# Seven products in the third block too, retention in one place from the sixth on, other PSUM banks for y, and SyncE's DMAs of the second block in another order

## The chip, the core and the metric

One core of a Trainium2 chip runs the kernel. The metric is the device time of one execution in microseconds (us). Five engines work beside each other, each with its own queue in program order: TensorE (PE, with its weight loads as PEld), VectorE (DVE), ScalarE (ACT), GpSimd (POOL) and SyncE (SP). SP computes nothing here; it issues nearly all DMAs.

## What is computed

Two layers, one behind the other. The first is a retention over 4 batches, 8 heads, 768 positions and a head size of 64; the second multiplies by `w_in` (512 x 2048), applies Mish, and multiplies by `w_out` (2048 x 512):

```python
for t in range(S):
    state = gamma[None, :, None, None] * state + np.einsum('bhd,bhe->bhde', k[:, :, t], v[:, :, t])
    y[:, :, t] = scale * np.einsum('bhd,bhde->bhe', q[:, :, t], state)
...
h = x @ w_in
sp = np.where(h > 20.0, h, np.log1p(np.exp(np.minimum(h, 20.0))))
g = h * np.tanh(sp)
return (g @ w_out).astype(np.float32)
```

Here `x` is `y` with the heads side by side: 3072 rows of 512. Inputs and output are float32; the products run in float16 with float32 sums.

## The kernel before, in words

**Chunks and blocks.** The positions are cut into 24 chunks of 128 (six to a batch). `BLOCKS` (L37) groups them: block 0 has chunks 0 to 3, and block b from 1 to 10 has chunks 2b+2 and 2b+3, so 256 rows of the output. Everything for a block b happens in one round of the loop at L817, in which the retention of block b+1 is put between the matrix products of block b.

**One chunk's way.** SP loads q, k and v of a chunk (`load`, L131; 256 KB each, buffers for 4 chunks of q and 6 of k and v). POOL casts them (`casts`, L217): q times a factor (L223), k times a constant (L228), v times a factor (L229); q and k share a tile `qk16` with 4 buffers. SP then issues a DMA transpose of that tile (`turn_by_dma`, L233 to L236), which gives `qkt`. `next_chunk` (L781) does this for one chunk and issues loads some chunks ahead.

**Retention of a pair of chunks.** `get_ready` (L465) has PE make the outer products `u_ps` (L401, from the casts) and the scores `at` (L394, from `qkt`), and then `settle` (L450) runs on DVE: `mid` (L436/L438), `suh` and `sth` (L445, L447), `mid` of the second chunk, and the masked scores `am` (L459). `leave` (L470) makes the last state. `retain` (L501) has PE write the past's part of `y_ps` (L475), and DVE reads one column of it (`seen`, L514) before `finish` (L519) adds the present's part and copies y to `xt` (L526 on DVE, L528 on ACT), the input of the next block's first product. With `later` given, `retain` also makes the outer products and scores of the block after the next in between the past's matmuls: that is "retention in one place".

**The two products of a block.** `g1` (L532) makes h in 8 steps of 8 matmuls of 256 columns (L541), and ACT applies Mish (L549). Blocks below `SEVEN` then make the second product plainly: 8 steps of 4 matmuls of 512 columns (L555), with `g2_out` (L559) copying the result to `osb` on DVE (L561). Blocks from `SEVEN` on cut the second product into 2 x 2 pieces and form it from seven products of 8 matmuls of 256 columns instead of eight (`seven`, L615; matmuls L635). This needs sums of pieces of `w_out` (`weight_sums`, L572: eight DVE instructions L588 to L591, made once, one after each step of the block before), sums of pieces of g for each block (`sums_a`, `sums_b`, `sums_c`: `gsum`, L604 to L613), three copies of partial results on ACT (`snap`, L641), and four additions or copies into `osb` on DVE (L647, L649).

**Order.** It is written by hand: `tc.manual_schedule()` keeps the program's order on each engine, and `plan_of` (L791) says after which step u of a block which piece of the other work is issued. `store_due` (L176) issues the stores of `osb` (L179) ahead of a step, when they are due. Before the change block 1 has `next_chunk` after steps 1 and 5, `get_ready` after 10, `retain` after 13, `finish` and `leave` after 14. Block 2 (the block before `SEVEN`) has them after 2, 8, 7, 12 and 13. Blocks from `SEVEN` (3) to `ONE` (6) have `get_ready` and `leave` after step 3, and `retain` and `finish` between the seven products; blocks above `ONE` have only `settle` and `leave`, after step 0.

**PSUM.** Three pools share eight banks: `mmps` (tag mm, 3 buffers), `pxps` (tag px, one) and `atps` (tag at, two of two banks each). `get_ready` takes both buffers of `atps`, one for `at`, one for `u_ps`. In blocks 1 and 2 y takes the buffer of `at` next, so it must wait until `am` has been read from there.

Of the kernel before, what the change touches and what calls it, by code (L numbers as in the profile page):

```python
# [10 lines left out]
FP32 = mybir.dt.float32  # L11
# [5 lines left out]
def kernel(  # L17
# [9 lines left out]
    nc = tc.nc  # L27
    B, H, S, D = q.shape
    d_model, d_ff = moe_w_in.shape
    P = 128  # L30
# [3 lines left out]
    HP = H // 2  # L34
# [3 lines left out]
    first = [sum(BLOCKS[:i]) for i in range(len(BLOCKS))]  # L38
# [26 lines left out]
    mmps = ctx.enter_context(  # L65
        tc.tile_pool(name="rn_mmps", bufs=3, space=bass.MemoryType.PSUM))
    pxps = ctx.enter_context(
        tc.tile_pool(name="rn_pxps", bufs=1, space=bass.MemoryType.PSUM))
    atps = ctx.enter_context(
        tc.tile_pool(name="rn_atps", bufs=2, space=bass.MemoryType.PSUM))  # L70
# [40 lines left out]
    loaded, cast, qkts, ats, ams, states, mids, us, ys = {}, {}, {}, {}, {}, {}, {}, {}, {}  # L111
    xts, gts, wins, wouts, wtmps = {}, {}, {}, {}, {}
    gtiles, tmats, gsums = {}, [], []
    SEVEN, ONE = 3, 6
    nload, ncast = [0], [0]
    stores = []

# [13 lines left out]
    def load(g):  # L131
        room(g)
        for n in range(3):
            load_one(g, n, nc.sync)

    def load_to(g):
        while nload[0] < min(g, NCK):
            load(nload[0])
            nload[0] += 1
# [249 lines left out]
    def pair_tile(pool, name, tag):  # L389
        return pool.tile([P, 2, 2, HP, D], FP32, name=name, tag=tag)  # L390
# [16 lines left out]
    def hold(blk):  # L407
        held[blk] = [pair_tile(atps, nm, "at") for nm in ("at", "u_ps")]
# [12 lines left out]
    def run(*streams):  # L421
        streams = [iter(x) for x in streams]
        while streams:
            for x in list(streams):
                fns = next(x, None)
                if fns is None:
                    streams.remove(x)
                else:
                    for fn in fns:
                        fn()  # L430
# [49 lines left out]
    def past_of(blk):  # L480
        a = first[blk]
        for j in range(2):
            qt = qkts[a + j][0]
            for s in range(2):
                st = mids[a + j] if s else states[a + j - 1] if (a + j) % NCH else None
                for i in range(HP) if st is not None else ():
                    yield [
                        lambda st=st, qt=qt, i=i, j=j, s=s, hh=hh: y_mm(
                            blk, i, hh, j, s, st[half(hh), i], qt[half(hh), i, half(s)])
                        for hh in range(2)]  # L490
# [10 lines left out]
    def retain(blk, later=None, spread=False):  # L501
        if spread:
            ys[blk] = [
                mmps.tile([P, 2, HP, D], FP32, name="y_ps", tag="mm") for _ in range(2)]
        else:
            y = pair_tile(atps, "y_ps", "at")
            ys[blk] = [y[:, s] for s in range(2)]
        if later is None:
            run(past_of(blk))
        else:  # L510
            hold(later)
            run(past_of(blk), ready(later, False))

        nc.vector.tensor_copy(seen, ys[blk][1][:, 1, 0, :1])  # L514
        if later is not None:
            run(ready(later, True))
            finish(blk, False)
# [40 lines left out]

    def g2_out(o_ps, blk, t, due, cols=slice(None)):  # L559
        osb = op.tile(list(o_ps.shape), FP32, name="osb", tag="osb")  # L560
        nc.vector.tensor_copy(osb, o_ps)  # L561
        if blk == 0:
            dst = out[:TB].rearrange("(p r) c -> r p c", r=CPB)[t]
        else:
            row0 = (first[blk] + t) * P
            dst = out[row0:row0 + P, cols]
        stores.append((due, dst, osb))
# [39 lines left out]
    def sums_b(blk):  # L607
        (_, _, s3, _), a11, _, a21, _ = sum_views(blk)
        nc.vector.tensor_tensor(s3, a11, a21, op=ALU.subtract)

    def sums_c(blk):
        (_, s2, _, s4), _, a12, _, _ = sum_views(blk)
        nc.vector.tensor_tensor(s4, a12, s2, op=ALU.subtract)  # L613

    def seven(blk, hooks, last):  # L615
        n, hf = NFB // 2, d_model // 2
        px = pxps.tile([P, hf], FP32, name="o_ps", tag="px")
        pb = mmps.tile([P, hf], FP32, name="o_ps", tag="mm")
        osb = [op.tile([P, d_model], FP32, name="osb", tag="osb") for _ in range(2)]

        def a(i, j):
            return lambda f: gts[blk, j * n + f][:, i * P:(i + 1) * P]

        def b(i, j):
            return lambda f: wouts[(i * n + f) // FPS][:, f % FPS, j * hf:(j + 1) * hf]

        def s(i):
            return lambda f: gsums[blk % 2][:, i - 1, f]

        def t(i):  # L630
            return lambda f: tmats[(i - 1) // 2][:, (i - 1) % 2, f]

        def mm(o_ps, x, w, first=False):
            for f in range(n):
                nc.tensor.matmul(  # L635
                    o_ps, x(f), w(f), start=first and f == 0, stop=f == n - 1,
                    skip_group_check=True)

        def snap(o_ps):
            x = op.tile([P, hf], FP32, name="snap", tag="snap", bufs=3)  # L640
            nc.scalar.copy(x, o_ps)  # L641
            return x

        def done(i, j, o_ps, plus=None):
            dst = osb[i][:, j * hf:(j + 1) * hf]
            if plus is None:
                nc.vector.tensor_copy(dst, o_ps)  # L647
            else:
                nc.vector.tensor_tensor(dst, o_ps, plus, op=ALU.add)  # L649
            row0 = (first[blk] + i) * P  # L650
            if last:
                nc.sync.dma_start(out[row0:row0 + P, j * hf:(j + 1) * hf], dst)

        mm(px, a(0, 0), b(0, 0), True)
        m1 = snap(px)
        mm(pb, a(0, 1), b(1, 0), True)
        sums_b(blk)
        done(0, 0, pb, m1)
        pe = mmps.tile([P, hf], FP32, name="o_ps", tag="mm")
        mm(pe, s(1), t(1), True)  # L660
        m5 = snap(pe)
        mm(px, s(2), t(2))
        u2 = snap(px)
        for fn, *args in hooks[0]:
            fn(*args)
        sums_c(blk)
        mm(px, s(3), t(3))
        done(1, 1, px, m5)
        for fn, *args in hooks[1]:
            fn(*args)  # L670
        mm(pe, s(4), b(1, 1))
        done(0, 1, pe, u2)
        mm(px, a(1, 1), t(4))
        done(1, 0, px)
        if not last:
            for i in range(2):
                row0 = (first[blk] + i) * P
                stores.append((1 + i, out[row0:row0 + P], osb[i]))
# [99 lines left out]
            for fn, *args in plan.get(u + 1, ()):  # L778
                fn(*args)

    def next_chunk(g):  # L781
        if g < NCK:
            cast_to(g + 1)
            turn_by_dma(g)
            if g < first[ONE] + 5:
                load_to(g + 3 if g < first[ONE] + 2 else g + 4)
            else:
                cast_to(g + 2)
                load_to(g + 5)

    def plan_of(blk):  # L791
        a = first[blk] + 4
        if blk >= SEVEN:
            plan = {u: [] for u in (0, 1, 3, 4, 7)}
            if blk > ONE:
                if blk + 1 < len(BLOCKS):
                    plan[0] = [(settle, blk + 1), (leave, blk + 1)]
            else:
                plan[3] = [(get_ready, blk + 1), (leave, blk + 1)]
            if blk >= ONE:  # L800
                plan[1] = [(next_chunk, a + 1)]
            else:
                ua, ub = (0, 4) if blk == ONE - 1 else (1, 7)
                plan[ua] += [(cast_to, a + 1), (next_chunk, a)]
                plan[ub] += [(cast_to, a + 2), (next_chunk, a + 1)]
            return plan
        early, then_seven = blk == 1, blk + 1 == SEVEN
        plan = {1: [(cast_to, a + 1)],
                (1 if early else 2 if then_seven else 4): [(cast_to, a + 1), (next_chunk, a)],
                (5 if early else 8): [(cast_to, a + 2), (next_chunk, a + 1)]}  # L810
        plan[10 if early else 7] = [(get_ready, blk + 1)]
        plan[13 if early else 12] = [(retain, blk + 1)]
        plan[14 if early else 13] = [(finish, blk + 1), (leave, blk + 1)]
        return plan

    first_block()
    for blk in range(1, len(BLOCKS)):  # L817
        n1 = NFB * BLOCKS[blk] // CPB
        last = blk + 1 == len(BLOCKS)
        plan = plan_of(blk)  # L820
        extra = weight_sums(0) + weight_sums(1) if blk + 1 == SEVEN else []
        for u in range(n1 if blk >= SEVEN else 2 * n1):
# [5 lines left out]
            else:  # L828
                t, part = divmod(u - n1, 4)
                if part == 0:  # L830
                    o_ps = mmps.tile([P, d_model], FP32, name="o_ps", tag="mm")
# [47 lines left out]
```

## Time and profile before

| what | value |
|---|---|
| median of 3 runs (lowest, highest) | 209.09 us (207.99, 209.56) |
| profiled execution: its time, its span | 208.58 us, 206.5 us |
| granted TensorE clock | 1.00 |
| PE busy | 198.6 us, 96% of the span |
| DVE, ACT, POOL busy | 118.7, 84.6, 79.2 us |
| second product, plain (L555), 128 matmuls | 30.0 us |
| second product, seven (L635), 192 and 128 matmuls | 24.0 and 15.3 us |
| DMA moved | 38.68 MB; 96704 packets of SP's queue |

The span runs from the first to the last instruction; the time is some 2.1 us longer. The page of the profile gives each engine's busy time, the DMA queues, and the chain of waits, which follows the execution back from its last instruction to what released each step. The timelines list the instructions of an engine in order of time (start, length, engine, line, operation, output<-inputs, count), with the idle time before a group and what ended it in square brackets. For a DMA, SP's row is the issue alone; when its data have landed is told apart, in the rows of its line.

### The profile page before, as it was taken

The numbers are of one execution on the slowest core, as the hardware profiler recorded it, in microseconds if no ns is written. First come the engines' busy times: TensorE is split into PE (matmuls) and PEld (weight loads), VectorE is DVE, ScalarE is ACT, GpSimd is POOL, SyncE is SP. The second block draws the span as 40 slices with busy tenths as digits, with TensorE's granted clock in tenths as the row PEclk, the third lists the DMA queues.
The fourth block names the chain that finished last, engine by engine and source line by source line (L and its number), as shares of the span: only waits on it lengthen the run. The fifth ranks groups of instructions, "written<-read, shape, count | busy, mean of one in ns | idle before, by whom it ended". The sixth has DMA issues, their size and how long they took to land.

```text
span 206.5 us, 5987 instructions
## 1 busy us (share of the span) xinstructions
PE 198.6 (96%) x2605; PEld 147.5 (71%) x2605; DVE 118.7 (57%) x211; ACT 84.6 (41%) x149; POOL 79.2 (38%) x82
## 2 busy tenths in 40 slices
PE   7999999999998899999999999999999999999993
PEld 2555444454864674788888887888888888888873
DVE  2697454267107999476388298296863853555152
ACT  2244665043530450352453452453363453542630
POOL 3246000426867266774466595098920000000000
PEclk9999999999999999999999999999999999999999
DMA  5999999999899999999999999999990500201102
GB/s 177 236 216 344 380 387 355 231 296 204 177 209 281 187 199 207 212 186 255 244 197 215 167 219 237 173 186 230 215 196 3 152 3 3 102 3 54 51 25 76
DMA packets 99993, 38.68 MB, mean 187 GB/s; under 512 B 90496, under 2 KB 94080, under 8 KB 99968
## 3 DMA queue, kind: packets, MB, share of 16 engines
q1 hardware_dynamic: 96704, 37.50, 89.0%
q10 hardware_dynamic: 3264, 0.81, 2.3%
q8 instruction: 20, 0.33, 0.7%
q14 instruction: 5, 0.04, 0.1%
HBM read 27.29 MB, written 6.29 MB: 163 GB/s over the span
## 4 chain that ended last, share of the span: by engine, by line
PE 75%; DVE 9%; DMA 6%; SPq 6%; ACT 1%; issue 1%; DVEq 0%; ACTq 0%
PE h_ps L541 37%; PE o_ps L635 22%; PE o_ps L555 8%; SPq L128 5%; PE y_ps L475 4%; DMA wi<-in_moe_w_in_dram 3%; DMA kf<-in_k_dram 3%; DVE gsum L604 2%; DVE am L459 2%; PE u_ps L401 2%; DVE sth L447 1%; DVE mid L438 1%; PE at L394 1%; DVE suh L445 1%; DVE gsum L605 1%
## 5 line engine op out<-in xcount | busy, mean ns | idle before, releaser
L541 PE MATMUL h_ps<-xt,win 128*128 128x256 f16 (+1 forms) x704 | 86.3, 282 | 1.1 <-ACT xt L528 0.5
L541 PEld LDWEIGHTS <-win 128*128 128x128 f16 x704 | 68.4, 98 | 17.3 <-issue 1.7
L549 ACT ACTIVATE g<-h_ps 128x512 f16<-128x512 f32 x96 | 57.3, 597 | 47.6 <-PE h_ps L541 47.6
L223 POOL TENSOR_TENSOR qk<-qf,qvs 128x512 f16<-128x512 f32 x20 | 22.1, 1107 | 50.0 <-DMA qf<-in_q_dram 34.0
L229 POOL TENSOR_TENSOR v<-vf,qvs 128x512 f16<-128x512 f32 x24 | 25.5, 1064 | 17.1 <-DMA vf<-in_v_dram 15.6
L555 PE MATMUL o_ps<-wout,g 128*128 128x512 f16 x128 | 30.0, 380 | 0.0
L228 POOL TENSOR_SCALAR qk<-kf 128x512 f16<-128x512 f32 x18 | 28.0, 1555 | 3.5 <-DMA kf<-in_k_dram 2.1
L635 PEld LDWEIGHTS <-gsum 128*128 128x128 f16 x256 | 23.9, 98 | 4.7 <-DVE gsum L604 1.1
L635 PE MATMUL o_ps<-tmat,gsum 128*128 128x256 f16 x192 | 24.0, 273 | 0.7 <-ACT snap L641 0.5
L555 PEld LDWEIGHTS <-g 128*128 128x128 f16 x128 | 11.7, 98 | 12.6
L635 PEld LDWEIGHTS <-g 128*128 128x128 f16 x192 | 18.8, 98 | 2.2
L604 DVE TENSOR_TENSOR gsum<-g 128x512 f16<-128x512 f16 x16 | 9.7, 603 | 14.2 <-ACT g L549 14.2
L528 ACT CAST xt<-y_ps 128x512 f16<-128x512 f32 x12 | 6.7, 588 | 25.7 <-DVE xt L526 16.0
L641 ACT COPY snap<-o_ps 128x256 f32<-128x256 f32 x24 | 8.9, 373 | 18.0 <-PE o_ps L635 18.0
L649 DVE TENSOR_TENSOR osb<-o_ps,snap 128x256 f32<-128x256 f32 x24 | 10.1, 422 | 9.1 <-ACT xt L528 3.1
L635 PE MATMUL o_ps<-wout,g 128*128 128x256 f16 x128 | 15.3, 273 | 0.0
L438 DVE TENSOR_TENSOR mid<-u_ps,sth 128x256 f16<-128x256 f32 x15 | 6.4, 423 | 10.7 <-PE u_ps L401 10.4
L249 PE MATMUL at<-ident 128*128 128x512 f16 (+1 forms) x34 | 10.8, 448 | 1.4 <-POOL ident L84 1.4
L459 DVE TENSOR_TENSOR am<-at,tri_half 128x1024 f16<-128x1024 f32 x9 | 10.9, 1214 | 0.0
L447 DVE TENSOR_TENSOR sth<-suh,gch 128x256 f16<-128x256 f32 x15 | 9.7, 649 | 0.6
L226 ACT ACTIVATE qk<-kf 128x512 f16<-128x512 f32 x6 | 3.8, 631 | 12.4 <-DMA kf<-in_k_dram 12.4
L436 DVE CAST mid<-u_ps 128x256 f16<-128x256 f32 x3 | 1.3, 422 | 12.9 <-PE u_ps L401 12.9
(79 smaller groups left out, 175.0 us busy)
## 6 DMA issues: line engine op xcount, KB each, us to landing
kf<-in_k_dram SPq DMA_DIRECT2D x23, 256.0 KB, 5.5
vf<-in_v_dram SPq DMA_DIRECT2D x23, 256.0 KB, 5.3
out_dram<-osb SPq DMA_DIRECT2D x22, 256.0 KB, 4.6
qf<-in_q_dram SPq DMA_DIRECT2D x19, 256.0 KB, 5.1
wt<-in_moe_w_out_dram SPq DMA_DIRECT2D x3, 1024.0 KB, 10.1
wi<-in_moe_w_in_dram SPq DMA_DIRECT2D x4, 512.0 KB, 7.2
wi<-in_moe_w_in_dram SPq DMA_DIRECT2D x2, 1024.0 KB, 10.8
qfirst<-in_q_dram SPq DMA_DIRECT2D x2, 512.0 KB, 4.9
```

The source lines that it names most:

```text
L128: queue.dma_start(loaded[g][n], (q, k, v)[n][b, :, c * C:(c + 1) * C].rearrange("h p d -> p h d"))
L223: nc.gpsimd.tensor_tensor(q16, qf, qs.unsqueeze(2).broadcast_to((P, H, D)), op=ALU.mult)
L228: nc.gpsimd.tensor_scalar(k16, kf, BOOST, None, op0=ALU.mult)
L229: nc.gpsimd.tensor_tensor(v16, vf, vs.unsqueeze(2).broadcast_to((P, H, D)), op=ALU.mult)
L249: nc.tensor.matmul(ats[g][:, 0, :m], ident, ident.unsqueeze(1).broadcast_to((P, m, P)), start=True, stop=True)
L447: nc.vector.tensor_tensor(st, su, gch, op=ALU.mult)
L459: nc.vector.tensor_tensor(am.rearrange("p a j i c -> p (a j i) c"), at.rearrange("p a j i c -> p (a j i) c"), tri_half.unsqueeze(1).broadc ...
L541: nc.tensor.matmul(h_ps[:, j], wins[s][f // 2][:, bp, f % 2 * P:(f % 2 + 1) * P], xts[blk][:, bp, :nt], start=(bp == 0), stop=(bp == NBP - 1))
L549: nc.scalar.activation(gt, h_ps, AF.Mish, scale=inv_boost3)
L555: nc.tensor.matmul(o_ps, gts[blk, fb][:, t * P:(t + 1) * P], wouts[s][:, f, cols], start=(fb == 0), stop=(fb == NFB - 1))
L604: nc.vector.tensor_tensor(s1, a21, a22, op=ALU.add)
L635: nc.tensor.matmul(o_ps, x(f), w(f), start=first and f == 0, stop=f == n - 1, skip_group_check=True)
```

## The change

Six things change; the line numbers are those of the kernel before.

1. `SEVEN` goes from 3 to 2: block 2 uses the seven products, and the eight weight sums are issued in block 1 instead of block 2. With this block 2 takes the plan of the blocks that follow it: `get_ready` of block 3 after step 3.
2. `ONE` goes from 6 to 5: block 5 makes the outer products and scores of block 7 inside its `retain`, and block 6 has no `get_ready`. Block 4 takes the plan that block 5 had; from chunk 14 on, loads are issued further ahead.
3. `retain` of block 1 (the only plain one left) puts y into one buffer of `mmps` and the one of `pxps` instead of `atps`.
4. In block 1 `g2_out` copies the first of the two results on ACT instead of DVE.
5. In block 1 chunk 8's transpose is issued after step 0, so ahead of the four stores of block 0, and without loads behind it; the load of chunk 10, the transpose of chunk 9 and the load of chunk 11 follow after step 2.
6. In the last block the product that gives `u2` is made before the one in `pe`.

SP's order in block 1 is thus: transpose 8, four stores, load 10, transpose 9, load 11, where it was four stores, transpose 8, load 10, transpose 9, load 11. On POOL the casts keep their order; on DVE the eight sums stand between the last `osb` copies of block 0 and `mid` of chunk 6.

```diff
--- before.py
+++ after.py
@@ -111,7 +111,7 @@
     loaded, cast, qkts, ats, ams, states, mids, us, ys = {}, {}, {}, {}, {}, {}, {}, {}, {}
     xts, gts, wins, wouts, wtmps = {}, {}, {}, {}, {}
     gtiles, tmats, gsums = {}, [], []
-    SEVEN, ONE = 3, 6
+    SEVEN, ONE = 2, 5
     nload, ncast = [0], [0]
     stores = []
 
@@ -503,8 +503,9 @@
             ys[blk] = [
                 mmps.tile([P, 2, HP, D], FP32, name="y_ps", tag="mm") for _ in range(2)]
         else:
-            y = pair_tile(atps, "y_ps", "at")
-            ys[blk] = [y[:, s] for s in range(2)]
+            ys[blk] = [
+                pool.tile([P, 2, HP, D], FP32, name="y_ps", tag=tag)
+                for pool, tag in ((mmps, "mm"), (pxps, "px"))]
         if later is None:
             run(past_of(blk))
         else:
@@ -558,7 +559,10 @@
 
     def g2_out(o_ps, blk, t, due, cols=slice(None)):
         osb = op.tile(list(o_ps.shape), FP32, name="osb", tag="osb")
-        nc.vector.tensor_copy(osb, o_ps)
+        if blk > 0 and t == 0:
+            nc.scalar.copy(osb, o_ps)
+        else:
+            nc.vector.tensor_copy(osb, o_ps)
         if blk == 0:
             dst = out[:TB].rearrange("(p r) c -> r p c", r=CPB)[t]
         else:
@@ -657,10 +661,14 @@
         sums_b(blk)
         done(0, 0, pb, m1)
         pe = mmps.tile([P, hf], FP32, name="o_ps", tag="mm")
+        if last:
+            mm(px, s(2), t(2))
+            u2 = snap(px)
         mm(pe, s(1), t(1), True)
         m5 = snap(pe)
-        mm(px, s(2), t(2))
-        u2 = snap(px)
+        if not last:
+            mm(px, s(2), t(2))
+            u2 = snap(px)
         for fn, *args in hooks[0]:
             fn(*args)
         sums_c(blk)
@@ -778,15 +786,14 @@
             for fn, *args in plan.get(u + 1, ()):
                 fn(*args)
 
-    def next_chunk(g):
+    def next_chunk(g, loads=True):
         if g < NCK:
             cast_to(g + 1)
             turn_by_dma(g)
-            if g < first[ONE] + 5:
-                load_to(g + 3 if g < first[ONE] + 2 else g + 4)
-            else:
+            if g >= first[ONE] + 5:
                 cast_to(g + 2)
-                load_to(g + 5)
+            if loads:
+                load_to(g + (3 if g < first[ONE] + 2 else 4 if g < first[ONE] + 5 else 5))
 
     def plan_of(blk):
         a = first[blk] + 4
@@ -804,14 +811,11 @@
                 plan[ua] += [(cast_to, a + 1), (next_chunk, a)]
                 plan[ub] += [(cast_to, a + 2), (next_chunk, a + 1)]
             return plan
-        early, then_seven = blk == 1, blk + 1 == SEVEN
-        plan = {1: [(cast_to, a + 1)],
-                (1 if early else 2 if then_seven else 4): [(cast_to, a + 1), (next_chunk, a)],
-                (5 if early else 8): [(cast_to, a + 2), (next_chunk, a + 1)]}
-        plan[10 if early else 7] = [(get_ready, blk + 1)]
-        plan[13 if early else 12] = [(retain, blk + 1)]
-        plan[14 if early else 13] = [(finish, blk + 1), (leave, blk + 1)]
-        return plan
+        return {0: [(cast_to, a + 1), (next_chunk, a, False)],
+                2: [(load_to, a + 3), (cast_to, a + 2), (next_chunk, a + 1)],
+                10: [(get_ready, blk + 1)],
+                13: [(retain, blk + 1)],
+                14: [(finish, blk + 1), (leave, blk + 1)]}
 
     first_block()
     for blk in range(1, len(BLOCKS)):
```

## The prediction

> Blocks (0 to 10) and chunks (0 to 23) are counted as the code counts them; block b from 1 on holds chunks 2b+2 and 2b+3, and times are us from the start of the span of the profiled execution.
>
> **What bounds the kernel now.** I read first the page's busy shares and slices: PE is busy 96% at a granted clock of 1.0 throughout, but the DMA row stands at 9 tenths as well until about 150. So I went on to the chain of waits for the length of each block on PE, then to SP's timeline with the landing times of its transposes, because PE can only be sped up where its data are there.
>
> The chain of waits (start, length, what) gives the blocks by the start of their first h_ps:
>
> ```profile
> 51.61 7.15 PE h_ps L541 x64
> ...
> 65.39 0.56 PE y_ps L475 x24
> ...
> 68.79 7.15 PE h_ps L541 x64
> ...
> 84.82 3.49 PE h_ps L541 x32
> ...
> 99.87 3.49 PE h_ps L541 x32
> ...
> 114.84 3.49 PE h_ps L541 x32
> ...
> 130.58 3.49 PE h_ps L541 x32
> ...
> 146.19 6.99 PE h_ps L541 x64
> ```
>
> Block 1 takes 17.18, block 2 16.03, block 3 15.05, block 4 14.97, block 5 15.74, block 6 15.61, and block 7 14.52 (its neighbour starts at 160.71). Blocks 3 on have seven products; 7 on have the retention in one place.
>
> SP's timeline around blocks 1 and 2 (start, length of the issue, line, kind):
>
> ```profile
> 59.42 1.50 SPq L128 DMA_DIRECT2D vf<-in_v_dram  x1
> 61.02 2.55 SPq L179 DMA_DIRECT2D out_dram<-osb  x4
> 63.66 2.53 SPq L235 DMA_TRANSPOSE qkt<-qk  x1
> 66.24 0.57 SPq L128 DMA_DIRECT2D qf<-in_q_dram  x1
> 66.91 1.27 SPq L128 DMA_DIRECT2D kf<-in_k_dram  x1
> 68.23 0.78 SPq L128 DMA_DIRECT2D vf<-in_v_dram  x1
> 69.10 2.40 SPq L235 DMA_TRANSPOSE qkt<-qk  x1
> ```
>
> SP has no gap. The transpose at 69.10 is chunk 9's; the row of its line in that window says when it landed:
>
> ```profile
> L235 SPq DMA_TRANSPOSE qkt<-qk x1: 2396/2396/2396, 69.1 to 69.1; - x1
> ...
> DMA to landing us min/median/max: 6.9/6.9/6.9
> ```
>
> So it landed at 76.0. PE's scores of block 3 (get_ready, which reads it) began at 76.14: 0.1 to spare. The table by windows (us, PE, PEld, DVE, ACT, POOL, PEclk, DMA share, GB/s) shows that the transfers, not the issues, were the limit:
>
> ```profile
> 60.00:64.00 4.00, 4.00 (x81) 2.01 (x79) 2.02 (x4) 0.00 (x0) 2.65 (x4) 1.00 1.11 268
> 64.00:66.00 2.00, 1.32 (x29) 0.77 (x27) 1.94 (x4) 0.00 (x0) 1.92 (x2) 1.00 1.04 352
> 66.00:68.00 2.00, 2.00 (x40) 0.94 (x39) 0.72 (x2) 0.00 (x0) 0.22 (x1) 1.00 1.32 86
> 68.00:72.00 4.00, 3.48 (x32) 2.87 (x30) 3.93 (x8) 2.18 (x4) 1.19 (x1) 1.00 1.29 221
> ```
>
> The share is over 1 in every window; from 66 to 68, with the transpose behind the four stores, only 86 GB/s moved.
>
> **Block 2 with seven products.** It loses 32 matmuls o_ps of 512 columns (4.42 for 20 in the chain, so 7.07) and gains 56 of 256 (3.49 for 32, so 6.10): 0.97 less PE work, and the 15.0 of blocks 3 and 4 in place of 16.03. ACT's three snaps (0.37 each) lie beside PE as in block 3. But get_ready of block 3 moves from step 7, between the two products, to step 3, four h_ps groups (3.6) earlier, and its scores need chunk 9's transpose.
>
> **Block 1 on PE.** y goes to other banks: the 0.68 of idle ahead of the y_ps row at 65.39 (released by DVE am, whose bank it took) goes; late next is nothing, as mid of chunk 7 is done at 64.20 and PE comes at 64.7. The present part then waits only for am (65.33) and runs behind the 4 o_ps, at 66.0 to 66.4. The two xt copies, one after the other before (DVE 67.43, ACT 68.15, released by DVE), run side by side as they do from separate tiles at 98.10 in block 3, so the 0.52 ahead of 68.79 goes too. Block 2 would start at about 67.3, 1.5 earlier. The first osb copy on ACT is bounded by xt (0.59) and snap (0.37): 0.6 in ACT's idle stretch of 8.76, and it takes 0.68 off DVE behind am. The second stays behind xt, suh and sth on DVE, done near 68.9; its bank is asked for by block 2's fourth h_ps group at 69.9: nothing.
>
> **The eight weight sums,** from block 2 to block 1: DVE is idle from 52.4 to 61.81 (the row before mid says 9.44). In block 2 the eight took 6.7 for seven and 1.51 for the last, 0.69 alone and up to 1.53 beside POOL; so about 8.2, done near 60.6, before the chain of mid at 61.8. POOL pays: its casts at 70.81 took 1.53, 1.81, 1.28 against 1.04, 1.49, 1.04 alone. The same 0.35 each on five casts (chunk 7 and two of chunk 8) less the 0.99 that POOL was idle at 57.48 puts chunk 8's k cast at 60.9 instead of 60.10, just as SP comes free (60.92). Ends: no delay, or each sum blocks POOL for its whole 0.69 (5.5 less 0.99: k cast at 64.6).
>
> **SP's order.** Before: stores, transpose 8, load 10, transpose 9. After: transpose 8, stores, load 10, transpose 9. Transpose 9 keeps the same work ahead of it. Ends for its landing L: with nothing queued, shortest issues (1.29; 4 by 0.53; 0.38, 0.50, 0.73) and the shortest landing (3.1) from 61.02, 69.1; with transpose 8 held for a k cast at 64.6, 78.4. I take 76.0 less what the stretch at 86 GB/s lost: its 0.17 MB needs 0.8 at the 210 around it, so 1.2, because the transpose no longer follows the stores: L = 74.8. That row is nearest, since DMA is full on both sides.
>
> PE reaches chunk 9's scores at 67.3 + 3.49 + 0.38 (u_ps) + 0.15 = 71.3 and waits 3.5. This swallows all that blocks 1 and 2 gain: from the end of the scores to the next block block 4 takes 10.81 (104.03 to 114.84), so block 3 starts at L + 0.15 + 10.81 = 85.8, where it was 84.82: **+1.0**. The chain mid, suh, sth runs on DVE during the wait, so gsum is not late in block 2.
>
> **Blocks 3 to 6.** ONE goes from 6 to 5. Block 3 stays 15.05. Block 6 becomes like block 7: 14.52. Block 5 becomes like block 6: 15.61. Block 4 takes block 5's plan; loads 16 and 17 go out together there and POOL's casts of both come free only with its own u_ps, so DVE's chain has POOL beside it as in block 5 (sth 0.80 and gsum 1.26 where they are 0.43 and 0.42 alone, 0.8 of wait): 15.74. Sum 60.92 against 61.37: **-0.4**; ends -1.2 (block 4 stays 14.97) and +0.3 (block 3 gets the wait too). SP's order changes with it: block 2's two stores go out at steps 1 and 2 of block 3, loads 16 to 23 a step earlier; transpose 17, now needed near the end of block 5 (about 128), landed at 128.0 before (issue 124.01, landing 4.0) with the same loads and one more store ahead; I cost it at nothing, and 0.5 if not.
>
> **Last block.** u2's product comes before pe: the 0.46 in front of the o_ps at 200.55 (released by ACT snap) goes, since pe's eight matmuls (0.87) then cover the copy (0.37): **-0.45**, ends -0.46 and 0.
>
> Sum: 1.0 - 0.4 - 0.45 = +0.15. The profiled execution took 208.58 (206.5 of span and 2.1 around it), so 208.7; the median of the runs, 209.09, is 0.5 above it, within their 207.99 to 209.56.
>
> **Rivals.** *The transpose is in time* (decided at L = 71.3): the reordering really frees the queue, as the shortest landings (3.1, 3.4) would have it. Block 3 then starts at 82.3, -2.5, in all -3.4: 205.2. For it speaks that SP's issues are long only because the queue is full; against it the share over 1 on both sides of 66. *Transpose 8 holds up SP* (slower): it stands at the head of SP's queue and waits for chunk 8's cast, with four stores, load 10 and transpose 9 behind it; POOL is slowed by the eight sums. At the upper end SP stands 3.6 idle, L = 78.4, block 3 +4.6, in all +3.7: 212.3; over 1% from a hold of 2.5 on. Against it: three casts lost 1.05 in block 2, not 4.5. [...]
>
> **How the numbers follow.** Forecast 0.62 (207.0 to 210.2: L from 74 to 76, blocks 3 to 6 between their ends), in time 0.20, strict turns 0.08, hold 0.10. A measurement here tells about 1% from no change: below 207.0 is faster (0.20 and 0.01 of the forecast's edge), above 211.2 slower (0.10 and 0.03 of edges and of turns), 0.66 within. The range 205.4 to 210.9 leaves out half of the first rival and the hold.
>
> **What would show it.** A PE gap of 2.5 to 4.5 in block 2 ahead of L394, released by the transpose; block 1 at 15.7; block 3 starting near 85.8; blocks 4 and 5 at 15.7 and 15.6, 6 at 14.5; no gap ahead of the last products. It is wrong if block 2 has no such gap, or if SP idles in front of transpose 8.

## The result and the profile after

| | before | after |
|---|---|---|
| median of 17 runs each (lowest, highest) | 208.98 us (207.99, 211.13) | 212.47 us (209.74, 214.58) |
| ratio, 95% interval | | 1.0123 [1.0093, 1.0154] |
| profiled execution: time, span | 208.58, 206.5 us | 213.24, 211.5 us |

The change makes the kernel slower by a good 1%; 208.7 and "the same" were forecast, and the median lies above the whole range. The ratio leaves the longest runs out, eight of the 17 of after and its profiled execution among them, so it is smaller than the quotient of the medians (1.0167).

The runs of after spread with the core's mean granted TensorE clock, which stands beside each run. The 21 executions of the changed kernel (17, and 4 of its repetition below) fall into three groups:

| mean granted clock | executions | time, us |
|---|---|---|
| 1.000 | 3 | 209.74 to 210.07 |
| 0.989 to 0.992 | 12 | 211.59 to 213.27 |
| 0.981 to 0.984 | 6 | 213.24 to 214.58 |

The kernel before stood at 0.997 to 1.000 in its runs beside the repetition. The means of the three groups are 209.9, 212.2 and 213.8 us. Without a loss of clock the kernel is about 1 us above the forecast and within its range; the 18 of 21 that lose clock are outside it.

The lengths of the blocks, from the start of one block's first h_ps to the next, in the profiled executions (the row "repeated" is the changed kernel once more, at clock 1.000; "forecast" follows the prediction's terms):

| block | 1 | 2 | 3 | 4 | 5 | 6 | 7 to the end |
|---|---|---|---|---|---|---|---|
| before | 17.18 | 15.87 | 15.04 | 14.98 | 15.74 | 15.61 | 60.45 |
| forecast | 15.7 | 18.5 | 15.05 | 15.74 | 15.61 | 14.52 | 60.0 |
| after | 15.78 | 21.61 | 15.04 | 16.28 | 16.68 | 14.67 | 59.83 |
| repeated | 15.78 | 17.75 | 15.04 | 15.97 | 16.69 | 14.68 | 59.82 |

From before to after: -1.40 in block 1, +5.74 in block 2, +1.30 and +0.94 in blocks 4 and 5, -0.94 in block 6, -0.62 from 7 on, and -0.06 in block 0; together +4.96, which is the spans' 211.45 - 206.48 = 4.97.

Line numbers are now those of the kernel after: L542, L556, L613, L639 and L653 are L541, L555, L609, L635 and L649 of before. Block 2 first. PE's timeline of after (start, length, engine, line, operation, output<-inputs, count, and in brackets the idle time ahead with what ended it):

```profile
67.33 3.67 PE L542 MATMUL h_ps<-xt,win 128*128 128x256 f16 x32
...
71.20 0.30 PE L394 MATMUL at<-qkt 64*64 64x64 f16 x16
75.72 0.43 PE L394 MATMUL at<-qkt 64*64 64x64 f16 x16 [4.22 <-DMA qkt<-qk]
76.08 5.70 PE L542 MATMUL h_ps<-xt,win 128*128 128x256 f16 x32
```

The first h_ps of block 2 starts at 67.33 (forecast 67.3), chunk 8's scores run at 71.20, and chunk 9's wait for their transpose, as forecast. The fourth line was not: the same 32 matmuls that took 3.67 ahead of the gap take 5.70 behind it. The table by windows (window, its length, then PE, PEld, DVE, ACT and POOL busy, PEclk, DMA share, GB/s) says why:

```profile
70.05:73.45 3.40, 1.45 (x57) 1.06 (x55) 1.89 (x4) 1.19 (x2) 1.31 (x2) 1.00 1.59 216
73.46:76.86 3.40, 1.14 (x20) 0.88 (x21) 1.03 (x2) 0.00 (x0) 2.30 (x2) 0.50 0.75 158
76.88:80.28 3.40, 3.40 (x18) 2.43 (x16) 2.14 (x3) 1.16 (x2) 2.47 (x2) 0.50 1.13 234
80.29:83.69 3.40, 3.40 (x33) 3.04 (x31) 2.78 (x5) 1.59 (x4) 1.30 (x2) 1.00 1.28 195
```

PE was granted half its clock from 73.46 to 80.28, for 6.83 us: from the middle of the gap until 4.6 behind its end. In the third row PE is busy throughout and gets 18 matmuls done, in the fourth 33. SP's timeline around the same place (start, length of the issue) has the transpose in question at 70.45; PE's wait for it ended at 75.7, which is taken as its landing:

```profile
59.26 1.06 SPq L128 DMA_DIRECT2D vf<-in_v_dram  x1
60.61 2.20 SPq L235 DMA_TRANSPOSE qkt<-qk  x1
62.91 2.82 SPq L179 DMA_DIRECT2D out_dram<-osb  x4
65.78 0.44 SPq L128 DMA_DIRECT2D qf<-in_q_dram  x1
66.30 0.76 SPq L128 DMA_DIRECT2D kf<-in_k_dram  x1
67.11 3.25 SPq L128 DMA_DIRECT2D vf<-in_v_dram  x1
70.45 3.17 SPq L235 DMA_TRANSPOSE qkt<-qk  x1
```

SP stands idle for 0.3 at most in front of transpose 8 (the issue ahead ends at 60.32, chunk 8's k cast at 60.58, the transpose is issued at 60.61), and the stretch at 86 GB/s of before has not gone; it has moved:

```profile
64.00:66.00 2.00, 2.00 (x32) 0.86 (x29) 1.35 (x3) 0.00 (x0) 1.92 (x2) 1.00 1.32 90
66.00:68.00 2.00, 2.00 (x44) 1.25 (x44) 1.39 (x3) 0.58 (x1) 0.11 (x1) 1.00 1.18 292
```

Then blocks 4 and 5. In the chain of waits of after, block 4 (h_ps from 104.15) has no longer PE work alone, but three steps of DVE:

```profile
104.15 3.49 PE h_ps L542 x32
...
112.20 1.19 DVE gsum L608
...
114.84 1.56 DVE gsum L613
116.40 0.35 DVE osb L653
```

PE's timeline shows what waited for them:

```profile
114.52 1.48 PE L639 MATMUL o_ps<-tmat,gsum 128*128 128x256 f16 x12 [0.43 <-DVE gsum L608]
...
116.79 0.31 PE L475 MATMUL y_ps<-qkt,sth 64*64 64x64 f16 x8 [0.54 <-DVE osb L653]
```

POOL's timeline has casts until 115.85:

```profile
113.20 1.52 POOL L228 TENSOR_SCALAR qk<-kf 128x512 f16<-128x512 f32 x1
114.81 1.04 POOL L229 TENSOR_TENSOR v<-vf,qvs 128x512 f16<-128x512 f32 x1
```

The step of L613 took 1.56, with a cast beside most of it; at 117.34, with POOL idle, the same form took 0.68 (L617). `osb` (L653) stands behind L613 on DVE, and the past's part of y waits until it has read its bank.

### The profile page after: what moved, and what is told of

Same layout as the page of the kernel before. It is cut to its first block, busy times and chain, and to the rows that moved or that the text cites. A ratio compares the mean times of both kernels' runs of the same rounds, so it can differ in the third digit from the quotient of the medians.

```text
span 211.5 us, 6051 instructions
## 1 busy us (share of the span) xinstructions
PE 199.1 (94%) x2629; PEld 150.8 (71%) x2629; DVE 122.4 (58%) x217; ACT 86.7 (41%) x154; POOL 79.2 (37%) x82
## 4 chain that ended last, share of the span: by engine, by line
PE 69%; DMA 11%; DVE 10%; SPq 6%; issue 1%; ACT 1%; DVEq 0%; ACTq 0%
PE h_ps L542 35%; PE o_ps L639 23%; SPq L128 5%; PE o_ps L556 4%; DMA wi<-in_moe_w_in_dram 3%; PE y_ps L475 3%; DMA kf<-in_k_dram 3%; DMA qkt<-qk 2%; DMA qf<-in_q_dram 2%; DVE am L459 2%; DVE sth L447 2%; DVE gsum L613 1%; DVE gsum L608 1%; PE u_ps L401 1%; PE at L394 1%
## 5 line engine op out<-in xcount | busy, mean ns | idle before, releaser
L542 PE MATMUL h_ps<-xt,win 128*128 128x256 f16 (+1 forms) x704 | 88.4, 286 | 0.8 <-DVE win L163 0.5
L542 PEld LDWEIGHTS <-win 128*128 128x128 f16 x704 | 69.4, 99 | 17.7 <-DVE win L163 1.1
L639 PEld LDWEIGHTS <-gsum 128*128 128x128 f16 x288 | 26.9, 98 | 4.9 <-DVE gsum L608 1.4
L639 PE MATMUL o_ps<-tmat,gsum 128*128 128x256 f16 x216 | 26.8, 273 | 0.9 <-DVE gsum L608 0.9
L639 PEld LDWEIGHTS <-g 128*128 128x128 f16 x216 | 21.1, 98 | 2.4
L556 PE MATMUL o_ps<-wout,g 128*128 128x512 f16 x96 | 22.6, 380 | 0.0
L645 ACT COPY snap<-o_ps 128x256 f32<-128x256 f32 x27 | 10.1, 372 | 20.6 <-PE o_ps L639 20.6
L653 DVE TENSOR_TENSOR osb<-o_ps,snap 128x256 f32<-128x256 f32 x27 | 11.4, 422 | 10.0 <-ACT xt L529 4.1
L639 PE MATMUL o_ps<-wout,g 128*128 128x256 f16 x144 | 17.2, 273 | 0.0
L556 PEld LDWEIGHTS <-g 128*128 128x128 f16 x96 | 8.8, 98 | 9.4
L394 PE MATMUL at<-qkt 64*64 64x64 f16 x288 | 6.4, 197 | 4.2 <-DMA qkt<-qk 4.2
L609 DVE TENSOR_TENSOR gsum<-gsum,g 128x512 f16<-128x512 f16 x18 | 9.2, 513 | 0.6
```

Of the source, the lines that this page charges most:

```text
L542: nc.tensor.matmul(h_ps[:, j], wins[s][f // 2][:, bp, f % 2 * P:(f % 2 + 1) * P], xts[blk][:, bp, :nt], start=(bp == 0), stop=(bp == NBP - 1))
L556: nc.tensor.matmul(o_ps, gts[blk, fb][:, t * P:(t + 1) * P], wouts[s][:, f, cols], start=(fb == 0), stop=(fb == NFB - 1))
L639: nc.tensor.matmul(o_ps, x(f), w(f), start=first and f == 0, stop=f == n - 1, skip_group_check=True)
```

## The experiments

The theory: the gap for transpose 9 in block 2 costs twice, as idle time and as lost clock; and the rest comes from DVE's order in blocks 4 and 5. The rivals: transfers at large, the copy of the retention into block 5 (`ONE`), and the sums or the SP order in block 1. All times are set against the kernel before on the same chip.

**again**: the changed kernel once more, unedited.

> The changed kernel once more, to see another execution of its own. [...]

Median 212.21 (209.84 to 212.54), ratio 1.0135 [1.0076, 1.0194]. The profiled execution is the one at clock 1.000, with PE's timeline

```profile
74.77 0.32 PE L394 MATMUL at<-qkt 64*64 64x64 f16 x16 [2.50 <-DMA qkt<-qk]
75.02 3.67 PE L542 MATMUL h_ps<-xt,win 128*128 128x256 f16 x32
```

A gap of 2.50, and the matmuls behind it at 3.67: block 3 starts at 85.85, where 85.8 was forecast. Block 1 had started 0.78 later than in after, and so the gap is 2.50 and not 3.5. The other three runs, at 0.991 to 0.992, took 211.98 to 212.54. So with the clock kept the forecast's sum for the start of block 3 comes out, and most executions do not keep it.

**spin**: 18 matmuls, whose result nobody reads, ahead of chunk 9's scores, so that PE is busy while it waits.

```diff
     def get_ready(blk):
         hold(blk)
-        run(ready(blk, True), ready(blk, False))
+        streams = [ready(blk, True), ready(blk, False)]
+        if blk == 3:
+            run(*[islice(x, 3 * HP) for x in streams])
+            keep = pxps.tile([P, HP, P], FP32, name="keep", tag="px")
+            for _ in range(18):
+                nc.tensor.matmul(
+                    keep, ident, ident.unsqueeze(1).broadcast_to((P, HP, P)),
+                    start=True, stop=True)
+        run(*streams)
         settle(blk)
```

> 18 matmuls of 512 columns on the identity (about 3.9 us) are put ahead of chunk 9's scores in block 2, into a bank nobody reads; nothing else changes. Theory A (PE's idle time drops the clock): no granted clock below 1.0 in block 2, the four h_ps groups behind the scores take 3.6 instead of 5.6, block 3 starts at about 87.1 instead of 89.1, and the time is about 2 us below that of the changed kernel: 210.2 to 211.2. Theory B (low clock from outside): the same time as the changed kernel, 212 to 213.5, with the low clock still there. If the wait for the transpose were not what ends the gap, the added matmuls would cost their 3.9 us: 216.

```profile
71.60 4.06 PE L473 MATMUL keep<-ident 128*128 128x512 f16 x18
75.59 0.32 PE L395 MATMUL at<-qkt 64*64 64x64 f16 x16
75.84 3.67 PE L551 MATMUL h_ps<-xt,win 128*128 128x256 f16 x32
```

Median 211.27 (210.75 to 212.97), ratio 1.0129 [1.0082, 1.0176]. The transpose, issued at 70.83, landed 4.7 later, so the added matmuls held up next to nothing. The scores start just as late as in after, but the matmuls behind take 3.67; three of four runs are at a clock of 0.999 or more. Beside after's profiled execution block 2 is 2.36 shorter; beside the repetition's median the whole gains only 0.94. Its three runs at full clock took 210.75 to 211.33, about 1 more than the three of the changed kernel at full clock (209.74 to 210.07). So the steps between the groups of after are not the clock alone. A later landing may go with them (75.7 in after's profile, 74.8 in the repetition's), but there is no trace of an execution of this kernel with one step, so this was not shown.

**t9_first**: transpose 9 ahead of chunk 10's load on SP.

```diff
-                2: [(load_to, a + 3), (cast_to, a + 2), (next_chunk, a + 1)],
+                2: [(cast_to, a + 2), (next_chunk, a + 1, False), (load_to, a + 4)],
```

> In block 1 SP issues transpose 9 ahead of load 10 instead of behind it; nothing else changes. Theory A (the landing of transpose 9 sets block 2, and its place in the queue sets the landing): issue at about 65.8, landing at 70 to 71, no gap ahead of chunk 9's scores, no low clock, block 3 starts at 82.4 to 83. Load 10 and with it transposes 10 and 11 come some 2 us later, so that block 3 may wait 1 to 1.5 for transpose 11. Time 207.5 to 209.5. Rival (DMA is so full that the order does not matter): transpose 9 lands at 73.5 or later, a gap of 2 or more is left, time above 210.5.

Median 208.05 (207.0 to 211.09), ratio 0.9947 [0.9921, 0.9973]. SP's and PE's timelines:

```profile
65.46 1.30 SPq L235 DMA_TRANSPOSE qkt<-qk  x1
```

```profile
71.19 0.46 PE L394 MATMUL at<-qkt 64*64 64x64 f16 x32
71.58 3.67 PE L542 MATMUL h_ps<-xt,win 128*128 128x256 f16 x32
...
78.20 1.48 PE L639 MATMUL o_ps<-tmat,gsum 128*128 128x256 f16 x12 [0.47 <-DVE gsum L608]
...
80.46 0.31 PE L475 MATMUL y_ps<-qkt,mid 64*64 64x64 f16 x8 [0.54 <-DVE osb L653]
```

The transpose is issued 5.0 earlier than in after and lands 4.1 behind its issue, at 69.6; the gap and the half clock are gone, block 2 takes 16.75, and the whole is 4 below after. So its place behind chunk 10's load made it late: 5.0 of the 6.1 is the later issue (the load's three issues take 4.6 of SP's time in after), the rest the longer way from issue to landing. Three of the ten runs took 210.16 to 211.09 at a clock of 0.998 or more, so the clock is not all that spreads runs here. Blocks 3 to 6 take 61.33 in this profile, where before has 61.37 and after 62.67, and block 4 takes 14.97 although `ONE` is 5: the lengthening of block 4 went with the late transpose. Two small gaps now show in block 2 that the long one had covered: sums of g, and the bank behind `osb`.

**one6**: `SEVEN, ONE = 2, 5` becomes `2, 6`.

> The changed kernel with retention in one place from block 6 to 7 on as before (ONE at 6 instead of 5). Theory A: block 2 is as in the changed kernel (gap, low clock); blocks 3 to 6 take about 61.4 as before the change instead of 62.7, because POOL's casts of chunks 16 and 17 no longer stand beside DVE's chain in block 4, so 1.3 less: 210.5 to 211.5. Rival (the longer blocks 4 and 5 come from the later start that the gap in block 2 gives them, not from ONE): blocks 4 to 6 together stay near 47.6, time as the changed kernel's.

Median 212.56 (212.27 to 212.94), ratio 1.0178 [1.0154, 1.0202], a miss: no gain. Its profile has a gap of 4.04 and 6.8 at half clock (the granted clock is 0.73 from 72 to 76 and 0.50 from 76 to 80, and the 32 matmuls behind the gap take 5.85). Blocks 4 to 6 take 47.08, where after has 47.63 and before 46.33: `ONE` at 5 gives 1.02 in block 6 and takes 1.57 in blocks 4 and 5. That is 0.55 of the 1.30 by which these blocks are longer than before; the rest, most of it in block 5 (16.41), is not `ONE`'s. Block 4 takes 14.99 here, behind the same late start, and 14.97 in t9_first, with `ONE` at 5 and no late start: it is long where both come together.

**plain3** and **plain3_one6**: only `SEVEN` back at 3, or `SEVEN` and `ONE` back at 3 and 6; banks, ACT's copy, SP's order in block 1 and the last block stay changed, and block 2, plain again, follows block 1's changed plan.

```diff
-    SEVEN, ONE = 2, 5
+    SEVEN, ONE = 3, 5
```

> The changed kernel with the third block's (block 2's) second product plain again (SEVEN at 3): the weight sums are back in block 2, and get_ready of block 3 stands behind two o_ps steps there; all else of the change is kept. Theory A (the seven products bring the scores of chunk 9 forward to where the transpose has not landed, and that alone makes the change slow): no gap in block 2 and no low clock; block 1 keeps its 15.8, block 2 takes 15.8 to 16.0, blocks 4 to 6 together 46.3 to 47.6; time 206.5 to 208.5, so 1 to 2 below the kernel before. Rival (the other parts, ONE and the new places of casts and sums, cost as much as the gap): 209 or more.

> As the run with the plain third block, and retention in one place starts where it started before the change as well: what is left of the change is y's banks, the osb copy on ACT, SP's order in the early blocks and the order of the last products. Theory A: block 1 at 15.8 and the end 0.4 to 0.6 shorter, so 207.0 to 208.0; against the run with the plain third block it shows what ONE at 5 is worth by itself: the same within 0.6. Rival (ONE at 5 is what costs in blocks 4 and 5): this one is 1 or more faster than the run with the plain third block.

plain3: 207.69 (206.86 to 210.45), ratio 0.9923 [0.9899, 0.9947]. plain3_one6: 207.04 (206.56 to 208.31), ratio 0.9915 [0.989, 0.9941]. Block 2 takes 15.99 in both, with block 1 at 15.85. So all that the change does besides block 2's seven products makes the kernel faster, by almost 1%, and `ONE` makes no difference that can be told.

**seven_only**: the kernel before with `SEVEN` alone at 2.

```diff
-    SEVEN, ONE = 3, 6
+    SEVEN, ONE = 2, 6
```

> The kernel before with one part of the change alone: seven products from block 2 on, with the weight sums in block 1; y's banks, SP's order, ONE and the last products as before. Block 2 starts at about 68.8, so its scores of chunk 9 come up at 72.9. Theory A: the transpose lands at 75.5 to 76.5 as it did, the gap is 2.6 to 3.6, on either side of where the clock fell in the executions so far (kept at 2.5, fallen at 4.0 and 4.2); with the clock kept block 2 takes 18 to 19 and the time is 210.5 to 212, with it fallen 2 more. Rival (the move of transpose 8 ahead of the stores is what delays transpose 9): it lands at 74.5 or earlier, time 209 to 210.

Median 211.31 (210.42 to 212.03), ratio 1.0114 [1.007, 1.0157]: by the ratio, block 2's seven products alone cost as much as the whole change. Blocks 3 to 6 take 61.43, as before (61.37). PE's timeline and the windows:

```profile
74.97 0.32 PE L394 MATMUL at<-qkt 64*64 64x64 f16 x16 [2.21 <-DMA qkt<-qk]
```

```profile
72.83:76.23 3.40, 1.26 (x26) 1.12 (x27) 2.76 (x5) 0.06 (x1) 1.32 (x3) 1.00 1.07 227
76.25:79.65 3.40, 3.40 (x19) 2.34 (x17) 2.19 (x5) 1.23 (x3) 3.24 (x3) 0.50 1.17 195
79.66:83.06 3.40, 3.40 (x33) 3.05 (x32) 2.29 (x4) 1.52 (x3) 1.39 (x2) 1.00 1.31 235
```

A gap of 2.21, shorter than the 2.50 that cost the repetition nothing, took half the clock for 3.41 us, from 1.3 us after PE was busy again. The 32 matmuls behind the gap took 5.33 instead of 3.66: one such step, with PE busy throughout, costs 1.67. The transpose, issued at 68.63 with SP's old order, landed at 74.93, later than the rival said and earlier than the theory did. The other edits of block 1 bring PE to chunk 9's scores sooner (71.5 in after, 72.8 here) and the transpose no sooner than 74.7, so what they save there turns into gap.

**t9_swap**: t9_first, and on DVE `osb` (L653) ahead of the sum of L613.

```diff
-        sums_b(blk)
         done(0, 0, pb, m1)
+        sums_b(blk)
```

> The kernel with transpose 9 ahead of load 10, and in the seven products the addition that empties pb (osb, L653) stands ahead of the sum s3 (gsum, L613) on DVE. Theory A (the gaps of 0.54 ahead of y_ps in the blocks in which POOL's casts stretch s3 to 1.56 come from y's bank, which is pb's and waits behind s3): both 0.54 gaps of that kernel (blocks 2 and 5) go, block 2 takes 16.2 instead of 16.75, block 5 16.15 instead of 16.69, time 1.0 lower: 206.5 to 207.2. Rival (s3 itself is then late for its product): the gap turns up ahead of the o_ps that reads s3, no gain.

Median 206.83 (206.38 to 207.4), ratio 0.9895 [0.9869, 0.992]. Both gaps of 0.54 are gone, block 2 takes 16.29 and block 5 15.97; what is left in PE's timeline are the waits for sums of g, and one of 0.20 for `seen` in block 4:

```profile
77.48 0.61 PE L639 MATMUL o_ps<-tmat,gsum 128*128 128x256 f16 x4 [0.37 <-DVE gsum L608]
...
78.57 1.48 PE L639 MATMUL o_ps<-tmat,gsum 128*128 128x256 f16 x12 [0.47 <-DVE gsum L608]
...
124.52 1.48 PE L639 MATMUL o_ps<-tmat,gsum 128*128 128x256 f16 x12 [0.43 <-DVE gsum L608]
```

**t9_swap_one6**: t9_swap with `ONE` at 6.

> As the run before in this list, with retention in one place starting where it started before the change. It prices ONE without the gap: if ONE at 5 saves the 0.4 to 0.6 by which blocks 7 on are shorter than block 4, this run is 0.3 to 0.6 slower than with ONE at 5; if the collisions of POOL and DVE take that back, it is the same or faster. Theory A: within 0.6 of it, 206.5 to 207.7.

Inconclusive: 208.95 (206.91 to 210.99), without a ratio. Its profile has two new waits, 1.22 for chunk 11's transpose in block 3 and 1.32 for a sum of g in block 5.

**t9_swap_cast6**: t9_swap with six buffers instead of four for `qk16`, so that POOL can cast earlier.

```diff
-name="qk16", bufs=4
+name="qk16", bufs=6
```

> The kernel with transpose 9 ahead of load 10 and pb emptied ahead of s3, and 6 instead of 4 buffers for the casts of q and k. Theory (POOL stands beside DVE's chain in blocks 4 and 5 because its casts of chunks 16 to 19 wait for that block's own u_ps to free a buffer): with 6 buffers the casts start when their loads land, some us ahead of the chain, the gap of 0.43 ahead of the gsum product in block 5 goes, blocks 4 and 5 take 15.0 to 15.4 each instead of 15.2 and 16.0: 205.8 to 206.6. Rival (the casts then only meet the chain of another block, or the loads are the limit): the gap stays or moves, 206.5 to 207.3.

Median 207.53 (205.93 to 209.37), ratio 0.9919 [0.9893, 0.9945]: nothing gained over t9_swap. The wait for gsum in block 5 is gone, but PE now waits for transposes:

```profile
125.83 0.22 PE L394 MATMUL at<-qkt 64*64 64x64 f16 x2 [0.51 <-DMA qkt<-qk]
...
141.94 0.22 PE L394 MATMUL at<-qkt 64*64 64x64 f16 x2 [1.33 <-DMA qkt<-qk]
```

**plain3_one6_swap**: plain3_one6 with `osb` ahead of L613.

> The run with the plain third block and ONE as before, with pb emptied ahead of s3. Theory: its gap of 0.49 ahead of y_ps in block 5 goes, so 0.3 to 0.5 lower: 206.4 to 206.9. It stands beside the run with seven products in block 2, transpose 9 first and the same exchange (206.83): if the two are the same within 0.4, the seven products in block 2 are worth nothing here, because the 0.97 of PE work that they save is taken back by the waits for gsum.

Median 206.22 (206.09 to 206.76), ratio 0.988 [0.9854, 0.9906]: the fastest of all here. Block 5 goes from 16.42 to 15.62, as the wait of 0.49 for `osb` is gone. PE's waits between 66 and 200 are now two, and the first, in block 3, is new; block 3 goes from 15.06 to 15.44:

```profile
97.13 1.05 PE L639 MATMUL o_ps<-wout,gsum 128*128 128x256 f16 x8 [0.32 <-DVE gsum L617]
124.38 1.49 PE L639 MATMUL o_ps<-tmat,gsum 128*128 128x256 f16 x12 [0.18 <-DVE gsum L608]
```

Against t9_swap, which has the seven products in block 2 and `ONE` at 5, it is 0.6 faster in the median, and the intervals of the two ratios overlap. So even with its transpose in time, block 2's seven products show no gain: the block takes 16.29 there and 15.98 here. In single executions it took less (15.71 in t9_swap_cast6; 15.22 in t9_swap_one6, whose block 3 then took 16.46), but neither run is faster as a whole. In t9_swap the 0.97 less PE work is used up by 0.84 of waits for gsum, whose DVE work is new in this block, and by small gaps that were not followed up.

## Why the prediction was wrong

- **Block 1: right.** 15.78 against 15.7; both gaps were y's bank and the copies to `xt`, and the eight weight sums fitted ahead of `mid`. They cost POOL about what was charged: chunk 8's k cast ended at 60.58, against 60.9.
- **Transpose 9: right in mechanism, and nearly in size.** It landed at 75.7 in the profiled execution and at 74.7 in the repetition, against L = 74.8. The 1.2 was taken off for a wrong reason: a stretch of 86 to 97 GB/s does not belong to "transpose behind the stores". It stands at 66 to 68 in before and seven_only, at 64 to 66 in after, and at 72 to 74 in the repetition and in plain3, two executions with the same order on SP as after. That L still came near 74.8 is luck in this term.
- **"This swallows all that blocks 1 and 2 gain ... so block 3 starts at L + 0.15 + 10.81 = 85.8": this step failed.** The 10.81 was taken from block 4, where PE runs without a gap. Behind the gap four h_ps groups took 5.63 in the chain instead of 3.60, so block 3 started 2.03 later than that sum by this alone (and 0.9 by L). The repetition, which kept its clock, started block 3 at 85.85. With spin the gap was filled and the 32 matmuls behind took 3.67; with t9_first there was no gap, and they took 3.67 too. I had read the granted clock as 1.0 throughout and never asked whether 3.5 of idle would leave it there. The price, by the runs, is 1.67 (seven_only, behind a gap of 2.21) to 2.03 (after, behind 4.22), and nothing in the repetition (2.50).
- **Blocks 3 to 6: the term -0.4 was mis-sized; it measured +1.30.** Block 3 was right (15.04) and block 6 nearly so (14.67 against 14.52). Block 4 took 16.28 against 15.74: less the 0.54 for y's bank behind `osb`, which block 5 of before did not have, the copied 15.74 is left, with 0.43 for gsum in it. But neither wait is there in t9_first, whose block 4 took 14.97 and whose blocks 3 to 6 took 61.33: the wait that I took over with block 5's plan does not come from the plan alone, and with the transpose in time the whole term is about nothing. These are single executions, and why block 4 has the waits only behind the late transpose was not settled. Block 5 took 16.68 against 15.61, with the same pair of waits, 0.43 and 0.53. t9_swap shows the second pair to be DVE's order: with `osb` ahead of L613 it goes in blocks 2 and 5, where t9_first has it. Why DVE is later here than in block 5 of before was not settled; POOL's casts fall beside other sums, and plain3_one6, with `ONE` at 6, has the wait as well (0.49).
- **Last block: right in kind.** From block 7 on -0.62 against -0.45.
- **The rivals.** *In time* did not come: the issues ahead of the transpose stayed long. It took t9_first to get there, and that gave 208.05, not 205.2, since other waits came up. *Transpose 8 holds up SP* hardly happened: SP was free at 60.32, the cast was done at 60.58 and transpose 8 issued at 60.61, a hold of 0.3 and not of 3.6. *Strict turns* of DVE and POOL, which have 0.08 in the chances, no run shows: beside the eight sums the five casts took 7.62 (6.10 by the times alone), and chunk 8's k cast ended at 60.58, where the kernel before has 60.10.

Set against the forecast's span of 206.65, after's 211.45 is 4.80 more: 3.14 at the start of block 3 (2.03 of clock, 0.9 of L, 0.2 around them), 1.75 in blocks 3 to 6, -0.17 from block 7 on, 0.08 of rounding. In 12 of the 21 executions the mean clock is 0.989 to 0.992, as with the one stretch of 3.41 at half clock in seven_only (0.991), and the time is near 212; after's profiled execution, with 6.83, has 0.984. At full clock it is 209.74 to 210.07, within the range; so it is the clock, with what goes along with it, that puts the median outside.

## What to carry to other kernels

When a change makes PE wait for data in the middle of a busy stretch, price the wait twice: its length, and the clock that the matmuls behind it may lose (here 1.7 us behind a gap of 2.21, 2.0 behind one of 4.22, nothing behind one of 2.50). When work moves earlier, look first at what its transfers have ahead of them in the queue: here one load moved behind one transpose gave back 4 us. A wait that you read in one block need not come along with its plan: block 4 had it in after and not in t9_first. And look at what stands behind a long step on the engine that frees a bank: exchanging two instructions on DVE was worth about 1 us by t9_first and t9_swap, and 0.7, with overlapping intervals, by the two runs with a plain block 2.

## What the runs showed of the hardware

The granted clock fell to half for 6.83 us in after (73.46 to 80.28) and for 3.41, half of that, in seven_only (from 76.25). The length of the gap did not decide: 2.21 cost 3.41 us of half clock, 2.50 nothing, 4.04 and 4.22 cost 6.8. In the 3.40 us just ahead of each fall PE was busy 1.45 (after) and 1.26 (seven_only); the stretches at half clock in which it was busy throughout (76.88 to 80.28, 76.25 to 79.65) were followed by full clock. Why the gap of 2.21 lowered the clock and that of 2.50 did not was not shown.

A stretch of 2 us at 86 to 97 GB/s with the DMA share above 1 was in five of the profiles (before 86, after 90, seven_only 92, again 95, plain3 97), around 64 to 74, and with the same order of issues at different places. In before, seven_only, again and after it begins 2.3 to 3.4 us behind the issue of a transpose (63.66, 63.54, 69.21 and 60.61), of chunk 8 or of chunk 9; t9_first has those transposes and no such stretch behind chunk 9's (209 GB/s at the least in the stretches of 2 us from 64 to 72). What makes it was not tried.
